# An attention and maxout feed-forward kernel: heads paired in natural order, transfers over 128 partitions, P V at the quad's end

## The chip, the cores and the metric

One core of one Trainium2 chip. The metric is the device time of one execution in microseconds, lower is better.

## The reference

Thresholded attention, then a feed-forward layer with the maximum of three products. Cut to what is computed:

```python
# q, k, v: (8 batches, 8 heads, 576 tokens, 64), float32; tau = 0.02
scores = matmul(q, k.T) / sqrt(64)
scores = where(scores >= max(scores) - tau, scores, -1e9)
attn = softmax(scores)                       # P in this document
x = (attn @ v) with heads side by side       # (4608, 512)
h = maximum(maximum(x @ w1, x @ w2), x @ w3) # w1..w3: (512, 768)
out = h @ w_out                              # (4608, 512), float32
```

## The kernel before

Work goes by **quads**, four heads of one batch: 16 quads. A quad has nine **steps**; one step makes two tiles of 128 query rows: scores on PE, their row maximum on DVE, the exponentials on ACT and DVE, the division on POOL, which gives P in bf16. P is then transposed by a DMA, because P V needs the keys on the partitions. A step has two **slots**, `2*n` and `2*n+1`, in which one piece of other work is put into the engines' order: transposes of the next quad's q and k, a P V product (`o_step`), or a piece of the feed-forward (`todo`: 18 hidden pieces and 5 output groups a batch). Each compute engine takes its instructions strictly in the order in which the source gives them (the class `_Ordered` sees to it). The sync queue (SP) issues nearly all transfers (loads, transposes of P and stores of the output).

The loads: 64 partitions each, because a pair of heads (0 and 2, say) is put on the two halves of the partitions. Ten DMA instructions a quad:

```python
def load(g, first=False):
    ...
    for i in range(2):
        rows = slice(64 * i, 64 * i + 64)
        h = slice(4 * qd + 2 * i, 4 * qd + 2 * i + 2)
        nc.sync.dma_start(out=L["q"][rows]....[:, :, 0:8, :], in_=rows_of(q, h)[:, :, 0:8, :])
        nc.sync.dma_start(out=L["q"][rows, 8:10], in_=rows_of(q, h)[:, :, 8, :])
        q2.dma_start(out=L["k"][rows]...., in_=rows_of(k, h))
    for r in range(2):
        ...                                   # v: four transfers, again 64 partitions each
```

P's transpose, on the same queue:

```python
def normalized(L, idx, z, sm):
    ...
    P = pp.tile([128, W], BF16, name="P")     # 6 buffers
    for n in range(2):
        pool.tensor_scalar(out=P[...], in0=z[...], scalar1=rs[:, n:n + 1], ...)
    nc.sync.dma_start_transpose(out=L["pt"][:, :, idx * 128:(idx + 1) * 128], in_=P)
```

The output group, from 3 buffers `ob`, in two stores of 64 partitions:

```python
            ob = hp_.tile([128, DM], F32, name="ob", bufs=3)
            ...
            scalar.activation(out=ob, in_=ps[:, :512], func=AF.Copy)
        ...
        for x in range(2):
            nc.sync.dma_start(out=dst[x], in_=ob[64 * x:64 * x + 64])
```

The plan of slots, and the weights, which POOL issues from its own queue:

```python
    for g in range(NQ - 2):
        for when, a in zip((10, 11, 14, 15), prep):
            at(18 * g + when, lambda g=g, a=a: transposed(Ls[g + 1], *a))
        early = g < 3
        at(18 * g + 18 + (9 if early else 3), lambda g=g: o_step(g, 0))
        at(18 * g + 18 + (15 if early else 8), lambda g=g: o_step(g, 1))
    ...
    for when, g, pr in ((11, y, 0), (13, y, 1), (19, z_, 0), (23, z_, 1)):
        at(e + when, lambda g=g, pr=pr: o_step(g, pr, 1))
    ...
        if wl and n in (14, 15, 16, 21, 22, 23, 27, 28, 29, 32, 33, 34):   # end of step n
            wl.pop(0)()
```

## Time and profile before

| | before |
|---|---|
| median of 3 runs | 534.41 us (533.86 to 535.54) |
| PE busy | 476.4 us, 90% of the span |
| first feed-forward matmul | at about 82 us |
| one steady batch (18 steps) | 60.7 us |

The second view is the sync queue's own timeline of the kernel before (start, length, queue, instruction, how many in a row):

```profile
67.58 0.62 SPq L134 DMA_DIRECT2D qm<-in_q_dram  x1
68.30 6.61 SPq L256 DMA_TRANSPOSE ptq<-P  x2
74.96 1.49 SPq L136 DMA_DIRECT2D qm<-in_q_dram  x1
76.50 0.60 SPq L137 DMA_DIRECT2D km<-in_k_dram  x1
```

Each line begins where the one above ends: the queue has no pause here. A load of 256 or 288 KB holds it for 0.6 us, one of 32 KB for 1.49 (0.6 elsewhere), and a transpose for over 3 on average here. From 20 to 140 us the queue is busy 108.4 of 120 us.

### The profile page before, as it was taken

How to read it: one execution, taken by the hardware profiler on the slowest of the kernel's cores; microseconds unless marked ns; L12 is line 12 of the kernel's file. 1: busy time of each engine (PE TensorE's matmuls, PEld its weight loads, DVE VectorE, ACT ScalarE, POOL GpSimd, SP SyncE). 2: the span in 40 equal slices, each digit the busy share in tenths (PEclk: the TensorE clock that was granted, in tenths of full speed). 3: DMA queues.
4: the chain of work that ended last, by engine and by line, in shares of the span. 5: the costliest groups of instructions: out<-in, count | busy, mean ns of one | idle time of the engine just before them, and what ended most of it. 6: DMA issues, size and time to landing. Idle time of an engine off the chain costs nothing.

```text
span 532.1 us, 10896 instructions
## 1 busy us (share of the span) xinstructions
PE 476.4 (90%) x3672; PEld 304.9 (57%) x3686; DVE 412.5 (78%) x992; ACT 401.3 (75%) x819; POOL 290.5 (55%) x386
## 2 busy tenths in 40 slices
PE   4877779996999899999999999999999989799896
PEld 3554546563556556665556655665566655566573
DVE  2899898975688877988699877988789896597542
ACT  1899897873877877787887878878878878586632
POOL 1687887582464655556565546647455566252310
PEclk9989899997999999999999999999999999899999
DMA  8799999999998698968887797977979566553652
GB/s 197 157 187 196 170 187 225 201 194 215 206 183 162 129 169 183 179 135 156 189 175 153 136 211 167 188 144 134 187 174 158 91 98 139 98 91 68 134 107 51
DMA packets 205560, 84.09 MB, mean 158 GB/s; under 512 B 178624, under 2 KB 193216, under 8 KB 205504
## 3 DMA queue, kind: packets, MB, share of 16 engines
q1 hardware_dynamic: 199648, 79.66, 78.3%
q0 software_dynamic: 5568, 3.15, 5.2%
q10 hardware_dynamic: 288, 0.59, 0.4%
q8 instruction: 29, 0.48, 0.4%
q14 instruction: 27, 0.22, 0.1%
HBM read 34.60 MB, written 9.44 MB: 83 GB/s over the span
## 4 chain that ended last, share of the span: by engine, by line
PE 39%; DVE 24%; ACT 10%; DMA 8%; issue 3%; POOL 3%; SPq 1%; ACTq 0%; DVEq 0%; POOLq 0%
PE ph L35 18%; PE sc L35 13%; DVE nm L35 12%; ACT z L35 7%; DMA ptq<-P 6%; PE o L35 5%; PE po L35 4%; DVE z L35 3%; DVE hm L35 2%; DVE hT L35 2%; POOL P L35 2%; DMA out_dram<-ob 2%; DVE bm L35 2%; DVE kt L35 2%; ACT ob L35 1%
## 5 line engine op out<-in xcount | busy, mean ns | idle before, releaser
L35 POOL TENSOR_SCALAR P<-z,rs 128x576 bf16<-128x576 f32 x288 | 213.6, 754 | 201.3 <-ACT z L35 171.8
L35 DVE TENSOR_REDUCE nm<-sc 128x1 f32<-128x576 f32 x288 | 216.0, 750 | 57.5 <-PE sc L35 56.8
L35 PE MATMUL sc<-kt,qs 64*128 64x256 f32 (+2 forms) x640 | 192.9, 446 | 15.8 <-ACT z L35 8.9
L35 ACT ACTIVATE z<-sc,bm 128x576 f32<-128x576 f32 x192 | 141.8, 739 | 84.7 <-DVE bm L35 64.9
L35 PE MATMUL sc<-kt,qt 64*128 64x320 f32 (+2 forms) x640 | 193.8, 454 | 6.5 <-ACT z L35 6.2
L35 PE MATMUL ph<-xt,w 128*128 128x288 bf16 (+2 forms) x1152 | 155.4, 287 | 4.6 <-ACT xt L35 3.4
L35 PEld LDWEIGHTS <-w 128*128 128x128 bf16 x1152 | 106.6, 98 | 58.1 <-issue 33.3
L35 ACT ACTIVATE z<-z 128x576 f32<-128x576 f32 x192 | 130.5, 683 | 0.0
L35 PEld LDWEIGHTS sc<-kt,qs 64*128 64x128 f32 (+1 forms) x640 | 94.1, 183 | 51.9 <-ACT z L35 31.5
L35 PEld LDWEIGHTS sc<-kt,qt 64*128 64x128 f32 (+1 forms) x640 | 93.5, 183 | 33.7 <-ACT z L35 23.7
L35 DVE SCALAR_TENSOR_TENSOR z<-z 128x576 f32<-128x576 f32 x96 | 75.2, 784 | 0.0
L35 ACT ACTIVATE z<-sc,nm 128x576 f32<-128x576 f32 x96 | 70.8, 738 | 1.9 <-DVE nm L35 1.9
L35 PE MATMUL o<-ptq,vb 128*64 128x288 bf16 (+3 forms) x660 | 47.5, 289 | 11.9 <-DMA ptq<-P 8.4
L35 POOL COPY qs<-qt 64x640 f32<-64x640 f32 (+2 forms) x64 | 48.3, 754 | 15.4 <-ACT qt L35 12.2
L35 PE MATMUL po<-wo,hT 128*128 128x512 bf16 (+1 forms) x274 | 51.8, 346 | 3.0 <-ACT ob L35 1.2
L35 DVE TENSOR_TENSOR hm<-ph,hm 128x576 bf16<-128x576 f32 (+2 forms) x54 | 36.9, 683 | 20.5 <-ACT hm L35 13.2
L35 PEld LDWEIGHTS <-vb 128*64 128x64 bf16 x660 | 34.5, 111 | 27.2 <-issue 14.7
L35 ACT ACTIVATE hm<-ph 128x576 bf16<-128x576 f32 (+2 forms) x54 | 32.1, 595 | 14.0 <-PE ph L35 13.9
L35 DVE TENSOR_TENSOR hT<-ph,hm 128x576 bf16<-128x576 f32 (+2 forms) x54 | 36.9, 683 | 3.6 <-PE ph L35 1.1
L35 PEld LDWEIGHTS <-hT 128*128 128x128 bf16 (+1 forms) x288 | 22.5, 102 | 29.5 <-issue 9.8
L35 ACT ACTIVATION_READ_ACCUMULATOR z<-z 128x1 f32 x192 | 38.7, 201 | 0.0
L35 DVE TENSOR_SCALAR bm<-nm 128x1 f32<-128x1 f32 x192 | 29.5, 154 | 6.6
(23 smaller groups left out, 235.4 us busy)
## 6 DMA issues: line engine op xcount, KB each, us to landing
km<-in_k_dram SPq DMA_DIRECT2D x30, 288.0 KB, 4.1
qm<-in_q_dram SPq DMA_DIRECT2D x32, 256.0 KB, 4.5
out_dram<-ob SPq DMA_DIRECT2D x64, 128.0 KB, 2.5
vm<-in_v_dram SPq DMA_DIRECT2D x32, 160.0 KB, 3.5
vm<-in_v_dram SPq DMA_DIRECT2D x32, 128.0 KB, 3.5
ptq<-P SPq DMA_TRANSPOSE x144, 3.7
w<-in_moe_w_dram POOLq DMA_DIRECT2D x9, 256.0 KB, 7.4
qm<-in_q_dram SPq DMA_DIRECT2D x32, 32.0 KB, 3.3
```

The costliest lines, as they stand in the source:

```text
L35: ins = fn(*a, **kw)
```

## The change

Its intent: pair neighbouring heads so that q, k and v each go over all 128 partitions; load v by pairs of tokens; store an output group with one transfer; put P V of a pair of heads later after the end of its quad (slots 16 and 19 in the first four quads and 10 and 13 in the others, instead of 9 and 15 in the first three and 3 and 8 in the others), where its P has long been transposed; hold each batch's last output group back until there is something to cover; and run 12 transposes of a constant first, so that the array is warm when the data comes. The core of the diff, cut at the marks:

```diff
-        for i in range(2):
-            rows = slice(64 * i, 64 * i + 64)
-            ...                                    # 6 loads of q and k, 64 partitions
+        for n, src, e in srcs:
+            e.dma_start(out=L[n][:, 8:10], in_=rows_of(src)[:, :, 8])
+        for n, src, e in srcs:
+            ...                                    # first quad: by rows of heads
+                e.dma_start(out=L[n]...[:, :, 0:8], in_=rows_of(src)[:, :, 0:8])
-        ...                                        # 4 loads of v, 64 partitions
+        for h in range(4):
+            nc.sync.dma_start(out=vm[:, h]..., in_=v[b, 4 * qd + h]...)      # 128 partitions
+        for r in range(2):
+            nc.sync.dma_start(out=vr[64 * r:64 * r + 64], in_=src[:, 8, 2 * r:2 * r + 2, :])
 ...
+        main = ps[:, 0:512].rearrange("p (i jj u x) -> p jj x i u", i=2, jj=2, x=2)
-            tensor.transpose(ps[:, 128 * j:128 * j + 128], couple(L, n, r, j), identf)
+            tensor.transpose(main[:, j // 2, j % 2] if j < 4 else ps[:, 512:640], couple(L, n, r, j), identf)
 ...                                                # kt, qt copied in two pieces for r == 0
-                dst = [rows[first], rows[first + 4]]
+                dst = rows[:, (0, 2, 1, 3)[c]:8:4]
+                nc.sync.dma_start(out=dst, in_=ob)  # was two of 64 partitions
 ...
-            todo.extend(ffn(b, xts[b], hTs[b], runs, chunks))
+            hids, outs = ffn(b, xts[b], hTs[b], runs, chunks)
+            todo.extend(hids + held + outs[:-1])
+            held[:] = outs[-1:]
 ...
-        early = g < 3
-        at(18 * g + 18 + (9 if early else 3), lambda g=g: o_step(g, 0))
-        at(18 * g + 18 + (15 if early else 8), lambda g=g: o_step(g, 1))
+        early = g < 4
+        at(18 * g + 18 + (16 if early else 10), lambda g=g: o_step(g, 0))
+        at(18 * g + 18 + (19 if early else 13), lambda g=g: o_step(g, 1))
 ...
-    for when, g, pr in ((11, y, 0), (13, y, 1), (19, z_, 0), (23, z_, 1)):
+    for when, g, pr in ((15, y, 0), (17, y, 1), (23, z_, 0), (25, z_, 1)):
 ...
+    for _ in range(WARM):                          # WARM = 12
+        tensor.transpose(warm[:, 0:128], identf, identf)
     Ls[0] = load(0, first=True)
-    ...                                            # first two heads, then scores, the others later
+    for r in range(2):
+        transposed(Ls[0], "q", r)
+        transposed(Ls[0], "k", r)
+        sc.append(scores(Ls[0], 0, r))
```

The number of loads a quad stays at ten (now 2 + 2 of q and k, 4 + 2 of v). Stores fall from ten to six a batch.

## The prediction

> **What bounds the kernel now.** I read the page first, then every engine's busy time by stretch, then the chain of waits and the timeline of the stretches that stood out. The page:
>
> ```profile
> span 532.1 us, 10896 instructions
> PE 476.4 (90%) x3672; PEld 304.9 (57%) x3686; DVE 412.5 (78%) x992; ACT 401.3 (75%) x819; POOL 290.5 (55%) x386
> PE   4877779996999899999999999999999989799896
> DMA  8799999999998698968887797977979566553652
> ```
>
> The tensor engine is full from slice 9 to the end; in the first eight slices it is not, and there the DMA row is at 9. So there are three stages, and the windows show them (columns: stretch, length, busy time of PE, weight loads, DVE, ACT, POOL, then clock, DMA share, GB/s):
>
> ```profile
> 4.00:6.00 2.00, 0.17 (x2) 0.20 (x3) 0.00 (x0) 0.00 (x0) 0.00 (x0) 1.00 1.07 224
> 45.00:60.00 15.00, 11.04 (x94) 7.22 (x93) 14.06 (x36) 13.88 (x29) 13.24 (x17) 1.00 1.18 179
> 120.00:150.00 30.00, 25.02 (x177) 14.46 (x177) 17.34 (x43) 18.46 (x39) 12.30 (x17) 0.89 1.05 200
> 274.20:334.93 60.73, 58.24 (x455) 36.52 (x457) 50.79 (x123) 49.72 (x102) 35.03 (x46) 1.00 0.82 167
> ```
>
> Up to 75 us there is no feed-forward work yet: DVE and ACT are full (14 of 15 us) and PE idles. From about 82 us, where the first feed-forward matmul stands in the timeline, PE carries all; one batch (18 attention steps) takes 60.7 us, 58.2 of them PE. Between 105 and 150 us something takes PE, DVE and ACT down together. The timeline of PE shows what (start, length, engine, instruction, then the idle time before it and what ended it):
>
> ```profile
> 111.23 0.74 PE L35 MATMUL o<-ptq,vb 128*64 128x256 bf16 x10 [0.79 <-DMA ptq<-P]
> 122.78 0.80 PE L35 MATMUL o<-ptq,vb 128*64 128x288 bf16 x10 [1.08 <-DVE nm L35]
> 126.86 1.41 PE L35 MATMUL o<-ptq,vb 128*64 128x288 bf16 x10 [3.28 <-DMA ptq<-P]
> 128.20 0.79 PE L35 MATMUL sc<-kt,qt 64*128 64x256 f32 x1
> 133.87 0.48 PE L35 MATMUL sc<-kt,qt 64*128 64x256 f32 x1
> ```
>
> P V stands in PE's order and waits for the transposed P; everything behind it waits too. After the longest wait the same score matmul takes 0.79 us, and 0.48 some microseconds later: the array went cold. Late in the run it happens once more, and the sync queue shows why early transposes are late: issuing one takes 4.45 us where the median is 1.33, so the DMA engines push back:
>
> ```profile
> 456.06 0.68 PEld L35 LDWEIGHTS <-vb 128*64 128x64 bf16 x10 [4.17 <-DMA ptq<-P]
> 59.18 4.45 SPq L256 DMA_TRANSPOSE ptq<-P  x1
> L256 SPq DMA_TRANSPOSE ptq<-P x144: 1242/1328/4771, 22.3 to 508.3; - x144
> ```
>
> **What the Trainium skill says.** "SBUF — State Buffer", section on the DMA port swizzle: partitions 0 to 63 reach 8 of 16 ports, and it gives 196 GB/s for them at 1 MiB against 328 over 128 partitions. The trace agrees as far as it can: every load here is over 64 partitions, and at 4 to 6 us, with a DMA share of 1.07 and only loads in flight, 224 GB/s move. "TensorE: Matmul & The Clock Gate", section on the HAM clock gate: the array starts at half clock and is released after some 3.4 us of activity. The trace agrees: score matmuls of 256 columns take 0.63 us until about 19 us and 0.38 later. The same page (Part 4) says that transposes may not count as activity, so whether 12 of them warm the array is open. The state buffer page also warns that non-contiguous PSUM access slows matmuls; the new transposes write every second column. No row of the old kernel shows that.
>
> **The change part by part.**
>
> *Loads over 128 partitions.* Per quad q, k and v are 1.77 MB. At 224 GB/s that is 7.9 us of all engines, at 328 GB/s (the skill's figure) 5.4: an estimate of 2.5 us less per quad. Early on a quad of nine steps lasts about 23 us. Late in the run (470 to 480 us) little but transposes moves, 0.91 MB in 10 us at a share of 0.53; a transpose is 0.295 MB, so one costs about 1.7 us and nine 15.5. Loads make 23.4, and the weights (5.2% of 532 us, 28 us, over four quads) another 7: over-full by some 7 us a quad. With the change it is over-full by about 5. So transposes will still lag while weights load; the relief is real but not complete. DMA instructions on the sync queue fall only by the 32 output ones that are merged; the queue isn't the bound.
>
> *P V at the quad's end.* This is what should remove the waits. A whole P V now stands at slots 16 and 19 after the quad's end in the first four quads and 10 and 13 later, two slots a step. The last P of a quad is issued about 2.5 steps after it, so early P V has 5.5 steps or more of slack (some 14 us at 2.6 us a step) against landing times of up to 11.2 us. Waits that should go: 1.08 + 3.28 + 0.79 and 0.41 (at 79.55 us), 5.6 us; the cold stretch after, about 1.5 us (a step's scores take 2.1 instead of 1.17 us, and an output group pays too); then 4.17 us plus a cold step of 1.0. In all 12 us, all of it on PE in the stage in which PE is the path. I count three quarters: **-9**. P V itself costs the same: 20 matmuls take 1.35 us now; with 512 + 64 columns, five pairs of 0.213 plus five of about 0.06 (30 late matmuls at 512.31 us take 1.52 us, of which pairs of 320 and 256 make 1.2) give 1.37.
>
> *First quad.* Before, the first maximum starts at 11.81 us, the second step's at 15.60 (the other two heads are transposed in between), the third's at 18.05. After: loads of 512 KB at about 330 GB/s land near 4.5 us instead of 5.8 and 7.3; transposes 1 us, ACT copies 0.9 (two of them), two POOL copies of 0.72; scores at 8, maximum at 8.8. The other row of heads goes through the same chain behind it: maximum at 11.9, second step at 12.7, third at 15.1. **-3**. The following steps are bound by ACT and DVE, so the warmed array gains only inside this chain.
>
> *Feed-forward later.* P V of batch 0 ends at slot 55 instead of 51, so feed-forward starts two steps later. Two steps without it cost 5.2 us, but their scores (2.3 us of PE) and DVE work are then behind us. Work is conserved; at equal balance this is +0 to +3. In a steady batch there are now three empty slots instead of one, and one step with P V and two transposes; the PE work per batch (18 x 1.17 scores, 18 x 1.03 hidden, 6.2 output, 5.4 P V, 5.6 transposes) stays at 56.8 us. One batch loses 3.9 us to imbalance; I give the new order **-1.5** in all over six batches, more than eaten if the heavy step stalls.
>
> *Copies split.* kt and qt of the first row of heads are copied in two pieces: from 640 -> 512 elements (0.803 -> 0.674 us on DVE, 0.696 -> 0.600 on ACT) a piece's fixed cost is 0.16 and 0.22 us; 16 times each gives 2.6 us DVE, 3.5 us ACT, beside PE except in the first three quads: +0.5.
>
> *Tail.* Counting the order of pieces: after the last step there are now 16 hidden pieces rather than 13, and one more small output group, +2.6 us, which the loop before is spared: 0. One 512-column group runs while the last hidden piece is copied instead of waiting for it: **-0.5** to -1.
>
> Sum: -9 - 3 - 1.5 + 0.5 - 1 = -14, from 534.4 to **520.4 us**.
>
> **Rivals.**
> 1. *The DMA engines stay the bound early.* For: over-full by an estimated 5 us a quad even after. Six P buffers let it lag by six steps, then POOL, ACT and scores stall (the old page of waits has this once, 1.9 us). Against: P V now tolerates the lag. Then only 4 to 5 of the 9 us are gained: 525 to 528.
> 2. *PE was the path, waits only moved it.* DVE and ACT are at 50 of 60.7 us per batch, so PE's gaps can be refilled only by PE; a gap taken out is time gained. But a wait for P could return late in the run, where P V has 2.5 steps less slack. Then 524 to 526.
> 3. *Strided PSUM writes slow 256 transposes.* Five take 0.77 us, paced by weight loads of 0.14; if each cost 0.1 us more, +25 us of PE: 545. I hold it unlikely (1 in 20), as the load paces them.
> 4. *All waits gone and a better balance:* the ledger of each step's longest engine falls by up to 6 us: 510.
>
> **Range and chances.** The 2% line is 523.7 us. The centre lies 3 us below it, and the four parts can each be off by 3 to 5 us, mostly independently, so some 9 us around the sum: 508 to 531 for 8 in 10. Faster by over 2%: 0.60; within: 0.36; slower: 0.04.
>
> **What would show it.** Loads: above 280 GB/s in the first 6 us, and transposes issued in under 2 us at 60 to 130 us. P V: no idle time over 0.5 us before it on PE, clock full from 120 to 150 us. First quad: third step's maximum near 15 us. Balance: a steady batch at 60 to 61 us. I am wrong if waits on the transposed P remain, if a steady batch takes over 61.5 us (heavy steps), or if transposes take over 0.2 us each.

## More of the kernel before

The prediction shows the lines that carry its argument. Two views are needed beside them. The first is the list of waits of the kernel before (engine, line, tile that waited, what it waited for: microseconds in total, how often, the longest):

```profile
PEld L35 <- DMA ptq<-P: 10.0, 5, 4.2
...
PE o L35 <- DMA ptq<-P: 8.4, 4, 3.9
...
ACT ob L35 <- DMA out_dram<-ob: 4.8, 2, 3.2
```

P V waits for the transposed P (`ptq`) four or five times, and twice ACT waits for an output buffer to be stored. The two PE rows overlap in time, since the weight loads stand beside the matmuls.

## The result

| | before | after |
|---|---|---|
| median, same rounds, 4 runs each | 534.97 us (533.86 to 536.11) | 520.48 us (519.57 to 521.27) |
| ratio | | 0.973, 95% interval 0.970 to 0.976 |
| span in the profile | 532.1 us | 518.0 us |

A ratio here is the mean time of one kernel's fast runs over that of the other's of the same rounds, so it is not quite the ratio of the medians. The time falls by 2.7%; 520.4 us were predicted.

The page of the changed kernel (span; busy time of the engines; PE in 40 slices, in tenths):

```profile
span 518.0 us, 11005 instructions
...
PE 475.1 (92%) x3700; PEld 292.1 (56%) x3700; DVE 411.6 (79%) x1008; ACT 402.6 (78%) x835; POOL 297.4 (57%) x418
...
PE   6777767999999999999999999999999999999996
...
```

No engine has clearly less to do: PE's busy time falls by 1.3 us only (with 2.8 us of warming transposes added). What went is idle time of PE, 55.7 us before and 42.9 after. The dips that the PE row had at slices 10, 14, 33, 35 and 38 are gone. The low part at the start is even one slice longer, because the feed-forward starts two steps later.

Its windows (stretch, length, busy time of PE, weight loads, DVE, ACT, POOL, clock, DMA share, GB/s):

```profile
4.00:6.00 2.00, 1.57 (x9) 1.39 (x9) 0.00 (x0) 0.04 (x1) 0.00 (x0) 1.00 1.05 351
...
45.00:60.00 15.00, 10.64 (x89) 5.92 (x90) 13.18 (x35) 13.14 (x29) 14.57 (x19) 1.00 1.03 165
...
120.00:150.00 30.00, 28.84 (x215) 16.62 (x214) 24.37 (x61) 25.58 (x54) 17.83 (x25) 1.00 0.91 208
269.54:330.05 60.51, 58.47 (x458) 35.24 (x456) 50.62 (x124) 49.92 (x104) 35.67 (x51) 1.00 0.79 170
```

At 4 to 6 us the loads now move 351 GB/s (224 before) with the same DMA share. From 120 to 150 us PE works 28.8 of 30 us, instead of 25.0. The steady batch takes 60.5 us, where it took 60.7. And at 45 to 60 us POOL has become full: 14.57 of 15 us.

The group of P V on its page (busy time, mean ns of one, idle time of the engine before them, and what ended most of it), and the sync queue's transposes (least, median and longest duration in ns):

```profile
L37 PE MATMUL o<-ptq,vb 128*64 128x64 bf16 (+2 forms) x544 | 39.9, 287 | 0.6 <-ACT z L37 0.6
```

```profile
L263 SPq DMA_TRANSPOSE ptq<-P x144: 1247/1326/4195, 21.3 to 491.7; - x144
```

PE's idle time before P V has fallen from 11.9 us (8.4 of it for a DMA) to 0.6, none of it for a DMA. A transpose's median is unchanged. (The chain of waits of the changed kernel can be followed back only to about 378 us, so it isn't used.)

To see *where* the time went I lined the two timelines up by attention steps: the start of the first row maximum of each step, after minus before.

| step | 0 | 3 | 14 | 27 | 28 | 36 | 40 | 48 | 132 | 134 | 143 | end of the span |
|---|---|---|---|---|---|---|---|---|---|---|---|---|
| us | 0.0 | -1.0 | -2.4 | -3.9 | -0.1 | -2.6 | -10.3 | -11.6 | -11.2 | -15.7 | -16.4 | -14.1 |

So: 1 us in the first quad; about 3 us more up to step 27, all lost again in one step; 11.5 us between steps 28 and 48 (88 to 166 us before, 88 to 155 after); nothing in the 84 steady steps; 5 us at the end of the attention; and 2 us lost in the tail.

Such a table misleads where work is put off, and here it is: the feed-forward starts two steps later. The windows of these stretches, before and then after, for steps 28 to 48 and 48 to 96, show it (columns as above):

```profile
88.20:166.20 78.00, 70.72 (x539) 44.42 (x539) 59.44 (x141) 55.98 (x115) 42.77 (x57) 0.96 1.10 196
166.20:329.90 163.70, 155.82 (x1220) 96.85 (x1224) 134.19 (x325) 132.58 (x269) 92.23 (x122) 1.00 0.81 164
```

```profile
88.10:154.60 66.50, 64.22 (x497) 39.30 (x493) 56.72 (x139) 54.45 (x113) 41.12 (x58) 1.00 1.05 202
154.60:318.30 163.70, 159.93 (x1264) 97.05 (x1260) 137.60 (x336) 134.80 (x281) 95.93 (x136) 1.00 0.81 165
```

In steps 28 to 48 PE is busy 6.5 us less; 4.1 us more of work are done in steps 48 to 96, in the same time, and 2.5 in the tail. PE's idle time (length less busy time, from such windows) doesn't have this fault:

| PE idle, us | up to step 28 | 28-48 | 48-96 | 96-132 | 132-143 | tail | sum |
|---|---|---|---|---|---|---|---|
| before | 24.1 | 7.3 | 7.9 | 5.1 | 5.6 | 5.7 | 55.7 |
| after | 25.6 | 2.3 | 3.8 | 5.4 | 0.3 | 5.5 | 42.9 |

So three stretches gain 4 to 5 us each, and one of them is a steady one.

The loss at step 28 is a wait that the prediction doesn't have. Timeline of PE, then of POOL, of the changed kernel:

```profile
83.63 0.53 PE L37 MATMUL sc<-kt,qs 64*128 64x320 f32 x1 [3.04 <-POOL qs L37]
```

```profile
77.98 0.79 POOL L37 DMA_DIRECT2D w<-in_moe_w_dram  x1
78.86 3.40 POOL L37 TENSOR_SCALAR P<-z,rs 128x576 bf16<-128x576 f32 x4
82.33 1.25 POOL L37 COPY qs<-qt 64x512 f32<-64x512 f32 x2
```

PE idles 3.04 us for `qs`, the second copy of q that POOL makes. POOL was behind: a weight load holds it for 0.79 us, then four divisions for P come first, 3.40 us; it is busy 15.5 of the 16 us from 66 to 82 (its weight loads counted; the kernel before has 15.5 there too).

One more quantity will decide the experiments: the **lag**, the time from the end of POOL's work on a P to the issue of its transpose on the sync queue. It is worked out from the traces, with the mean time that the issue itself takes:

| lag, mean (longest) us; mean issue us | steps 10-20 | 20-30 | 30-40 |
|---|---|---|---|
| before | 3.3 (8.1); 2.34 | 10.9 (13.9); 2.31 | 6.9 (11.5); 1.71 |
| after | 1.6 (3.6); 1.89 | 2.1 (3.2); 2.09 | 1.1 (2.5); 1.91 |

Before, a transpose waits 11 us for its turn on the queue. After, 2 us. From step 50 on both kernels have about 0.4 us, and an issue takes 1.40 and 1.48 us. The lag varies even where the source doesn't: two of the experiments below do not differ from the kernel before up to step 36 and have 7.0 and 8.1 us at steps 20 to 30; four others hardly differ from the changed kernel there and have 2.1 to 4.4.

### The profile page after: what moved, and what is told of

Its sections match the earlier page's. It is cut to its first block, busy times and chain, and to the rows that moved or that the text cites. A ratio compares the mean times of both kernels' runs of the same rounds, so it can differ in the third digit from the quotient of the medians.

```text
span 518.0 us, 11005 instructions
## 1 busy us (share of the span) xinstructions
PE 475.1 (92%) x3700; PEld 292.1 (56%) x3700; DVE 411.6 (79%) x1008; ACT 402.6 (78%) x835; POOL 297.4 (57%) x418
## 2 busy tenths in 40 slices
DMA packets 213272, 84.09 MB, mean 162 GB/s; under 512 B 186336, under 2 KB 200928, under 8 KB 213216
## 3 DMA queue, kind: packets, MB, share of 16 engines
q1 hardware_dynamic: 207088, 79.66, 73.9%
## 5 line engine op out<-in xcount | busy, mean ns | idle before, releaser
L37 PE MATMUL sc<-kt,qs 64*128 64x256 f32 (+2 forms) x640 | 189.3, 438 | 22.3 <-POOL qs L37 10.9
L37 PE MATMUL sc<-kt,qt 64*128 64x320 f32 (+2 forms) x640 | 190.3, 447 | 8.7 <-ACT z L37 8.5
L37 PEld LDWEIGHTS sc<-kt,qs 64*128 64x128 f32 (+1 forms) x640 | 90.1, 178 | 57.5 <-ACT z L37 28.7
L37 PEld LDWEIGHTS sc<-kt,qt 64*128 64x128 f32 (+1 forms) x640 | 89.8, 178 | 41.1 <-ACT z L37 34.6
L37 POOL COPY qs<-qt 64x640 f32<-64x640 f32 (+1 forms) x64 | 48.4, 756 | 11.4 <-ACT qt L37 8.2
L37 PE MATMUL o<-ptq,vb 128*64 128x64 bf16 (+2 forms) x544 | 39.9, 287 | 0.6 <-ACT z L37 0.6
L37 PEld LDWEIGHTS <-vb 128*64 128x64 bf16 x544 | 21.2, 112 | 21.1 <-issue 10.3
```

Source lines behind the costliest of these rows:

```text
L37: ins = fn(*a, **kw)
```

## The experiments

Twelve kernels, in three jobs of four, all correct. The kernel before took 532.82, 532.76 and 533.49 us (medians) in the three jobs. Ratios are to the kernel before as it was timed with the job. The changed kernel has 0.973, but it was not run again in these jobs, and the kernel before took 534.97 us beside it; so differences to the changed kernel of about 0.5% or less aren't resolved.

Theory A, as predicted: P V now stands late enough, so its waits go. Rival B: the waits go because transfers over 128 partitions move faster. Rival C, formed when A fell: the sync queue is a server of instructions in order, it was behind, and the change let it keep up.

### P V of one more quad late, in the old kernel

```diff
-        early = g < 3
+        early = g < 4
```

> The kernel before with one number changed: P V of quad 3 stands at the late slots (9 and 15 of the next quad) that quads 0 to 2 already have, instead of 3 and 8. Theory A (the gain is P V leaving the slots at which the transposed P is not there yet): the wait of 1.08 + 3.28 us at 122 to 127 us and the cold array after it go, 5 to 8 us faster, 527 to 529 us. Theory B (the wider loads made the transposes land earlier): the wait only moves, under 2 us.

Measured: 531.42 us, ratio 0.999 (0.995 to 1.002). The wait of P V near 126 us went, and step 40 came 8.1 us sooner. Then most of the time was given back. Timeline of ACT:

```profile
133.98 0.60 ACT L35 ACTIVATE ob<-po 128x512 f32<-128x512 f32 x1 [4.37 <-DMA out_dram<-ob]
```

The next output group finds no free buffer for 4.37 us: the stores of earlier ones stand in the sync queue behind loads and transposes. Two steps later the gain is 3.8 us. It stands at 5.7 us again at step 48, but that is work put off: from there to step 96 PE is busy 159.5 us instead of 155.8, and from step 96 on 2.2 us are left. What follows: theory A holds for the wait itself, and it isn't what bounds that stretch. Taking away the wait at P V mostly turned it into a wait at the next thing that needs the same queue.

### The late slots of the last two quads too, in the old kernel

```diff
-        early = g < 3
+        early = g < 4
-    for when, g, pr in ((11, y, 0), (13, y, 1), (19, z_, 0), (23, z_, 1)):
+    for when, g, pr in ((15, y, 0), (17, y, 1), (23, z_, 0), (25, z_, 1)):
         at(e + when, lambda g=g, pr=pr: o_step(g, pr, 1))
-    for when, g, pr in ((28, y, 0), (32, y, 1)):
+    for when, g, pr in ((33, y, 0), (34, y, 1)):
```

> As the last one, and the split P V of the last two quads at the new kernel's later slots (15, 17, 23, 25, 33, 34). Theory A: the wait of 4.17 us near 452 us goes as well, 9 to 12 us faster than the kernel before, 522 to 525 us, so nearly the whole gain of the change without its loads, layout, first quad or held group. Theory B: less than half of the gain, above 528 us.

Measured: 527.24 us, ratio 0.990 (0.987 to 0.994), 5.6 us less than before by the medians. Nearly all of what it gains over the last experiment comes between steps 132 and 134. The wait for the transposed P in its list of waits:

```profile
PEld L35 <- DMA ptq<-P: 0.6, 2, 0.4
```

The last experiment still had 4.7 us there, the longest 4.3. So late in the run, where the queue is not behind, theory A holds in full: P V stood too close to its P, and moving it gains the 4 to 5 us. These slots explain 1.0% of the 2.7. They are not all of the new ones: slots 16 and 19 of the first four quads, 10 and 13 of the others, and with them the later start of the feed-forward, were never tried with the old loads. They remain a rival for steps 28 to 96.

### The new kernel with its large loads cut into halves of 64 partitions

```diff
-                e.dma_start(out=L[n].rearrange("p (r c) d -> p r c d", r=2)[:, :, 0:8], in_=rows_of(src)[:, :, 0:8])
+                for s_ in (slice(0, 64), slice(64, 128)):
+                    e.dma_start(out=L[n][s_].rearrange("p (r c) d -> p r c d", r=2)[:, :, 0:8], in_=rows_of(src)[s_, :, 0:8])
 ...                                        # the first quad and v in the same way
```

> The new kernel with its q, k and v transfers cut into two of 64 partitions each (the 64-token remainders left as they are). Theory A: P V has slack for late transposes, so at most 3 us slower than the new kernel, under 524 us. Theory B: the transposes come late again, P V or the P buffers wait, 6 us or more slower, above 526 us. In either case the bandwidth in the window of 4 to 6 us should fall from 351 to about 225 GB/s.

Measured: 537.55 us, ratio 1.010 (1.007 to 1.014): 17 us slower than the changed kernel, and slower than the old one. The lag at steps 20 to 30 is 14.5 us. Its waits:

```profile
ACT ob L37 <- DMA out_dram<-ob: 11.8, 2, 11.2
...
POOL P L37 <- DMA ptq<-P: 9.5, 5, 4.9
...
PE o L37 <- DMA ptq<-P: 5.2, 1, 5.2
```

Output buffers, P buffers and P V all wait, with P V in its late slots. At 4 to 6 us it moves 229 GB/s, as expected. But this kernel has two differences, the halves *and* 16 loads a quad instead of ten. The control is needed.

### The same number of loads, each over 128 partitions

The same transfers are cut in two the other way: q and k by the row of heads, v by columns.

```diff
-                e.dma_start(out=L[n].rearrange("p (r c) d -> p r c d", r=2)[:, :, 0:8], in_=rows_of(src)[:, :, 0:8])
+                for s_ in range(2):
+                    e.dma_start(out=L[n][:, 10 * s_:10 * s_ + 8], in_=rows_of(src)[:, s_, 0:8])
 ...                                        # the first quad and v in the same way
```

> Control for the run with half-height transfers: the new kernel with just as many DMA instructions, but each still over 128 partitions (q and k cut by the row of heads, v by columns into 512-byte pieces). If the partitions made the half-height run slow (ratio 1.010 of the kernel before): ratio near the new kernel's 0.973, up to 0.980. If the number of DMA instructions on the sync queue did it: 1.00 or more.

Measured: 536.27 us, ratio 1.005 (1.000 to 1.010), as slow as the halves within the intervals. At 4 to 6 us it moves 274 GB/s, less than the 351 of the larger transfers. Every large load is over 128 partitions, and the DMA engines have *less* to do than in the old kernel over the whole run (72.7% of their time in the hardware queue, 78.3% before). One wait shows how the loss arises: ACT, then the sync queue just before.

```profile
157.81 0.60 ACT L37 ACTIVATE ob<-po 128x512 f32<-128x512 f32 x1 [8.55 <-DMA out_dram<-ob]
```

```profile
140.18 6.31 SPq L267 DMA_TRANSPOSE ptq<-P  x4
146.60 3.47 SPq L146 DMA_DIRECT2D vm<-in_v_dram  x5
...
151.62 1.95 SPq L146 DMA_DIRECT2D vm<-in_v_dram  x3
153.61 1.29 SPq L150 DMA_DIRECT2D vr<-in_v_dram  x2
155.00 0.63 SPq L332 DMA_DIRECT2D out_dram<-ob  x1
```

The store of an output group that was ready at about 142 us is issued at 155.00, behind transposes and ten pieces of v. Its 0.63 us were never the trouble; its place in the queue was. Rival B falls as the cause of this slowness: the *number* of loads makes it, and 64 partitions add about 0.5%, which the overlapping intervals don't resolve.

### Eight tiny loads more a quad

The direct test of rival C: instructions without bytes. Eight loads of 1 KB, over 16 partitions, into a tile that nothing reads.

```diff
+        dm = ld.tile([16, 8, 16], F32, name="dm")
+        for x in range(8):
+            nc.sync.dma_start(out=dm[:, x], in_=q[b, 4 * qd, 16 * x:16 * x + 16, 0:16])
```

> The new kernel with eight loads of 1 KB more per quad on the sync queue (into a tile that nobody reads): 0.5% more bytes. If the number of DMA instructions on that queue is what sets the lag of the transposes in steps 10 to 40: lag near 10 us in steps 20 to 30 (2.1 in the new kernel, 10.9 before), ratio 0.995 to 1.01, as with the control. If the control was slow for its small packets: ratio under 0.980.

Measured: 560.24 us, ratio 1.048 (1.043 to 1.053): 40 us more than the changed kernel, for 0.15 MB added to 84.09. Its sync queue early on, then all the tiny loads (least, median and longest duration in ns, first and last start), then its waits:

```profile
17.08 3.84 SPq L150 DMA_DIRECT2D dm<-in_q_dram  x8
```

```profile
L150 SPq DMA_DIRECT2D dm<-in_q_dram x128: 311/419/1766, 7.3 to 201.6; - x128
```

```profile
POOL P L37 <- DMA ptq<-P: 30.2, 14, 4.5
...
ACT ob L37 <- DMA out_dram<-ob: 21.3, 1, 21.3
```

Eight loads of 1 KB hold the queue for 3.84 us, 0.48 each, where a load of 512 KB holds it for 0.4 to 0.6. The lag grows to 15 us and more, POOL runs out of P buffers (30 us) and ACT waits 21.3 us for one store. The DMA engines are less busy meanwhile (share 0.90 at 80 to 140 us, against 1.06 in the changed kernel). So instructions alone, without bytes or wide ports, can make this queue the bound. How much one costs doesn't follow: the build did not put eight into each quad but all 128 before 202 us, 51 of them in the nine steps from 36 on, which take 57.8 us instead of 30.3. One rival is settled by the traces: each transfer on this queue also waits for the one eight ahead of it to land, but from 20 to 140 us that one had landed before the queue was free in all cases but one here (0.8 us), and in all in the changed kernel.

### The outputs stored in two halves again

```diff
-                nc.sync.dma_start(out=dst, in_=ob)
+                for s_ in range(2):
+                    nc.sync.dma_start(out=dst[32 * s_:32 * s_ + 32], in_=ob[64 * s_:64 * s_ + 64])
```

> The new kernel with each output transfer cut into two of 64 partitions, as before. The half-height run showed ACT waiting 11 us at a time for an output buffer. If merging the output transfers is part of what keeps output buffers free: ratio 0.978 to 0.985 and a wait of ACT on the output DMA of 3 us or more. If only the loads matter: 0.973 to 0.976.

Measured: 521.03 us, ratio 0.979 (0.976 to 0.983), 0.7% over the changed kernel's ratio. The lag stays small (3.0 us at steps 20 to 30), and ACT waits for a store 0.7 us, not the 3 that were expected with such a ratio. Its trace is already 2.4 us behind the changed kernel at step 20, before the first store, and 0.8 us more at the end. So what merging the stores is worth isn't resolved; it is small.

### Nothing held back

```diff
-            todo.extend(hids + held + outs[:-1])
-            held[:] = outs[-1:]
+            todo.extend(hids + outs)
```

> The new kernel without the held back output group: each batch's output groups follow its hidden pieces at once. If holding back matters at the end only (a filler while the last hidden piece is copied, and one 0.8 us group more after the loop): within 1.5 us of the new kernel, either way.

Measured: 521.62 us, ratio 0.980 (0.977 to 0.983). By the spans the held group is worth 1.1 us (519.1 against 518.0), by the ratios 0.7%. Its size between these is not settled. In its trace PE idles 2.2 us more in steps 48 to 132, so the held group is worth something in the steady batches too.

### Both rows of heads transposed before the first scores

```diff
     for r in range(2):
         transposed(Ls[0], "q", r)
         transposed(Ls[0], "k", r)
+    for r in range(2):
         sc.append(scores(Ls[0], 0, r))
```

> The new kernel with both rows of heads of the first quad transposed before the first scores, so that the second row's transposes do not stand behind scores that wait for POOL. Second step's first maximum 11.5 us instead of 14.67. If the early stage is bound by ACT and DVE throughout, 2 to 3 us faster at the end (ratio 0.968); if POOL and the DMA engines set the pace by 66 to 88 us, the gain is lost there (0.973).

Measured: 517.97 us, ratio 0.972 (0.969 to 0.975), not distinguishable from the changed kernel. Yet the first steps come about as early as the prediction had wanted. Timeline of DVE:

```profile
9.30 0.76 DVE L37 TENSOR_REDUCE nm<-sc 128x1 f32<-128x576 f32 x1 [0.64 <-PE sc L37]
```

The first maximum starts at 9.30 us, not 11.82, and the third step 4.5 us sooner than in the old kernel. Against the changed kernel it leads by 3.6 us at step 3, by 1.9 from step 20 on and by 1.6 at the end. About half of what is gained at the start is taken back between steps 14 and 20, where the weight loads begin on POOL.

### No warming

```diff
-    warm = slot("warm")
-    for _ in range(WARM):
-        tensor.transpose(warm[:, 0:128], identf, identf)
```

> The new kernel without the 12 warming transposes. In the new kernel the first scores run at 0.38 us (warm) but those of the second row, at 12.3 us, at 0.74 again (cold), so the warming lasts only for one chain of 4 us. Expected: the first copy of q later by 1 us at most, ratio within 0.3% of the new kernel's 0.973.

Measured: 521.17 us, ratio 0.976 (0.971 to 0.981). The first steps come 0.7 us later and are level by step 28. The warming is worth nothing that these runs resolve. But in these two traces it does warm the array. The first scores with it (the changed kernel), then without:

```profile
8.40 0.48 PE L37 MATMUL sc<-kt,qs 64*128 64x256 f32 x1 [1.93 <-POOL qs L37]
```

```profile
8.48 0.79 PE L37 MATMUL sc<-kt,qs 64*128 64x256 f32 x1 [1.40 <-POOL qs L37]
```

Up to there PE has run nothing but transposes in both.

### The weights earlier

```diff
-        if wl and n in (14, 15, 16, 21, 22, 23, 27, 28, 29, 32, 33, 34):
+        if wl and n in (2, 4, 6, 8, 10, 11, 13, 15, 17, 20, 22, 29):
```

> The new kernel with the weights loaded from step 2 on, one load every second step, instead of in steps 14 to 34. POOL is full from 66 to 82 us (15.6 of 16 us), and 3.04 us of PE wait for its copies of q at 83.63 us. If POOL's issuing of weight loads (0.79 us each) and their traffic make that stall: the four microseconds lost between steps 26 and 28 stay, 3 to 5 us faster (ratio 0.964 to 0.968). If the traffic only moves to an earlier time: 0.973 or slower.

Measured: 525.05 us, ratio 0.986 (0.984 to 0.989): slower by 1.4%. The lag of the transposes falls to 0.8 us, and it doesn't help: steps 6 to 26 run 2 to 9 us later than in the changed kernel. A miss that tells something: once the queue keeps up, less lag is worth nothing, and the first stage has no room for the weights. Whether it is POOL's time for issuing them or their traffic (DMA share 1.29 at 45 to 60 us, against 1.03) isn't separated.

### The weights later

```diff
-        if wl and n in (14, 15, 16, 21, 22, 23, 27, 28, 29, 32, 33, 34):
+        if wl and n in (22, 23, 24, 26, 27, 28, 30, 31, 32, 34, 35, 36):
```

> The new kernel with the weight loads in steps 22 to 36 instead of 14 to 34; the feed-forward part now starts at step 28. Loading them earlier cost 1.4%, because each load takes POOL 0.79 us in the stage in which POOL is nearly full. If POOL is a bound before step 28, six loads moved behind it save up to 4.7 us: ratio 0.963 to 0.967. If the loads only meet the transposes at a worse place (DMA share over 1 in steps 28 to 36), P V or the first hidden layer waits for a DMA: 0.975 or slower.

Measured: 518.22 us, ratio 0.970 (0.966 to 0.974). The loss at step 28 shrinks from 3.8 to 2.3 us, and the steady lead over the old kernel is 14.5 us in its trace instead of 11.5. The ratio's interval overlaps that of the changed kernel, so the gain of the time is likely, not shown.

### Both of the last two that helped

The weights later and both rows transposed first:

```diff
+    for r in range(2):
         sc.append(scores(Ls[0], 0, r))
 ...
-        if wl and n in (14, 15, 16, 21, 22, 23, 27, 28, 29, 32, 33, 34):
+        if wl and n in (22, 23, 24, 26, 27, 28, 30, 31, 32, 34, 35, 36):
```

> The last one together with the first quad's transposes ahead of its scores (that alone: second step 3.5 us sooner, but ratio only 0.972). If POOL and weight traffic before step 28 ate that gain, both add up: 2 us or more faster than the late weights alone, ratio 0.958 to 0.963. If the gain is lost in any case: equal to the late weights alone.

Measured: 515.76 us, the lowest median of all, ratio 0.967 (0.960 to 0.974). The runs scatter from 513.68 to 521.18 us; the profiled one is the slowest, and in it the lag is back at 8.6 us at steps 20 to 30 and 5.7 us are lost at steps 40 to 44. From step 3 to 36 it leads the late weights alone by 3.4 to 3.9 us, so with the weights out of the way the gain of the first quad lasts. That the queue falls behind in one run of this program and not in another is a guess; only one of its runs was traced. Best version here, with an interval that still touches the changed kernel's.

## Why the prediction was right, and where its working was not

The total was right to 0.1 us, and that is partly luck: the start was put too low by 1.5 to 4.5 us and the gain of the new order too low by about 3. I compare by PE's idle time, since PE's busy time hardly changed.

**P V at the quad's end (-9 predicted, about -10 measured).** The waits did go, all of them: idle time before P V is 0.6 us, and the clock is full from 120 to 150 us. PE's idle time falls by 5.0 us in steps 28 to 48 and by 5.3 in steps 132 to 143. The reason given, slack of slots, is shown only for the late part, where moving P V alone takes PE's idle time from 5.6 to 1.0 us. In the early part, moving P V of the quad that waited left about 2 us of gain in the trace (0.1% in the times, not resolved); most of the rest went into a wait for the output buffers.

**The step that failed: "the queue isn't the bound".** The prediction counted the bytes and the DMA engines' share, and set the sync queue aside because its instructions hardly fall in number. Adding instructions to the queue costs 16 us (the same bytes in 16 loads over 128 partitions) or 40 us (128 loads of 1 KB), and in the second of these the DMA engines are less busy than in the changed kernel (share 0.90 against 1.06 at 80 to 140 us; with the 16 larger loads it is 1.22). The reckoning that I should have made, with the durations of the traces at steps 20 to 30: before, ten loads of 0.67 us and nine transposes of 2.31 us make about 27 us of queue for nine steps, which last 28 us there. After, 10 x 0.68 + 9 x 2.09 is about 26, for 28 us again. With 16 loads of 0.6 it is about 28. These are estimates, and they leave little room in either kernel: from 20 to 140 us the queue is busy 108.4 us before and 106.5 after. It stood at its capacity and now stands just under it.

The DMA engines are not out of the matter. From step 50 on a transpose's issue takes 1.40 us, and nine of these with ten loads make 19 us, which would fit. It is the longer issue early on, where the engines' share is above 1 (1.18 at 45 to 60 us before, 1.03 after), that fills the queue. That the engines "push back", as the prediction says, fits these numbers; no run isolates it.

What gave the relief is not isolated either. The count of loads didn't fall, a load is issued no faster at steps 20 to 30, and the stores begin only later. A transpose's issue there takes 2.09 us instead of 2.31. The wider loads are the likely cause. They do save about what was estimated: the hardware queue's packets took 78.3% of 532.1 us before and 73.9% of 518.0 after for the same 79.66 MB, 34 us less or 2.1 a quad, where 2.5 were predicted. But at equal count, with the queue overfull in both, 64 or 128 partitions differ by about 0.5%, unresolved. Two experiments are missing: the old pairing of heads loaded over 128 partitions in ten transfers, which its layout doesn't allow, and the old loads with all the new slots.

**The first quad and the later feed-forward (-3 and 0 to +3 predicted, together +1.5 measured).** Up to step 28 PE idles 25.6 us instead of 24.1. The first maximum was put at 8.8 us and came at 11.82. Timeline of DVE of the changed kernel:

```profile
11.21 0.69 DVE L37 COPY kt<-tp 128x512 f32<-128x512 f32 x1 [3.81 <-PE tp L37]
11.82 0.75 DVE L37 TENSOR_REDUCE nm<-sc 128x1 f32<-128x576 f32 x1
```

The first maximum stands in DVE's order behind the *second* row's `kt` copy, which waits 3.81 us for transposes that stand in PE's order behind the first row's scores. The prediction drew two chains side by side; the program has them in one order on two engines. Taking the scores out of that order gives 9.30 us. About half of the gain so made is given back before step 28: the assumption that the start is on the path that sets the end held for 1.6 of its 3.6 us.

**A new wait.** The 3.04 us for POOL at step 28 are in none of the rivals. POOL's page share was 55%, an average over stages; in the first stage it is full. Later weights shrink the loss, which supports the reading.

**Balance (-1.5 predicted, about -4 measured).** PE's idle time in steps 48 to 96 falls from 7.9 to 3.8 us. It is as low in the two variants with 16 loads (3.8 us), where the queue is far behind until step 48, and not in the old kernel with the late slots of the last quads (7.6 us). So it belongs to the rest of the new order or the layout, not to the queue; without the held group it is 5.1 us. In steps 96 to 132 nothing is gained (5.1 and 5.4 us).

**Copies split, strided transposes, tail.** The split copies are not separable from the first stage. The strided writes of the transposes cost nothing: the median for q is 273 ns in both kernels. The tail is 2.3 us longer, as its pieces were counted (+2.6), and the loop is spared as much: PE is busy 2.5 us more in the tail and no more in all. So the term 0 stands; the -0.5 to -1 beside it is not seen (PE idles 5.5 us in the tail, 5.7 before).

**Rivals.** The first named the right place (transposes still late, P and output buffers next), and what part its DMA engines have in it is open; it expected only 4 to 5 of the 9 us. The second, a wait for P returning late, did not happen. The third, slower transposes, did not either.

**Of the tests named:** loads above 280 GB/s, no wait before P V, full clock and the steady batch came out as written. Transposes issued in under 2 us did not quite (2.08 on average at 60 to 130 us), nor did the third step's maximum near 15 us (17.08). Three readings were off without effect: PE is full from slice 7 of the page, not 9; the 30 late matmuls take 1.57 us, not 1.52; and the score matmuls show the half clock at the start but not the 3.4 us, since the full clock is granted from 19.35 us on, 13.5 us after PE's first work.

## What to carry to other kernels

Treat a DMA queue like an engine: sum the durations of all its instructions, stage by stage, and compare that sum with the stage's length before looking at bytes or at the DMA engines' share. When a wait for a transfer goes away, ask what else stands in the same queue; in the old kernel it mostly moved to the output buffers. When you line two timelines up, ask whether the same work is done by then; idle time of the bounding engine tells more. Draw each engine's order when you price a start-up chain, since two chains that share engines in one order are not side by side.

## What the Trainium skill lacked or had wrong

- "DMA: Bandwidth & Descriptors", section "Issuing engines are not separate DMA queues", says that the time to initiate a DMA is usually small relative to the DMA itself. For one transfer that holds here (0.46 us of issue for a 512-KB load of q, 4.4 us to its landing). But the sum decides: a load holds the sync queue about as long at 1 KB (median 0.42 us) as at 512 KB, a transpose for 1.33 us at the median and up to 4.8; 128 loads of 1 KB cost 40 us of 520. The page has no rule to sum a queue's instructions. Its section "Rules for kernel authors" advises against two transfers to disjoint partition halves, because they share the same DMA engines. The advice holds (1.010 against 0.973), but in this kernel mostly for another cause: as many transfers over 128 partitions each give 1.005.
- "SBUF — State Buffer", section "Door 1: The DMA port swizzle": confirmed in direction, 351 GB/s over 128 partitions against 224 over 64 when only loads are in flight. The page doesn't say that this need not show in a kernel whose queue is full. Its note that non-contiguous PSUM access significantly slows matmuls was not seen for PE's transposes: writing every second column left their median at 273 ns.
- "TensorE: Matmul & The Clock Gate", Part 4, says that the full clock doesn't engage for transposes. For this kernel's transposes it does: in the changed kernel the clock is granted in full from 5.78 us on, after transposes alone, they themselves go from 0.42 to 0.27 us, and the first scores take 0.48 us. Without the 12 warming ones the full clock comes at 16.88 us, and the first scores take 0.79. Nine of the ten traced kernels with warming have the full clock before 7 us; the tenth has it at 17.07.
